# All eight buffers of weight parts at one remainder of 256 bytes, and four buffers of weight sums for five

## The chip, the core and the metric

The kernel runs on one core of a Trainium2 chip. TensorE (PE in the profile; PEld are its weight loads) multiplies, VectorE (DVE), ScalarE (ACT) and GpSimd (POOL) do the rest on data in SBUF, and SyncE (SP) issues the transfers. The metric is the time of one execution on the device in microseconds (us), smaller being better. Of the kernel before there are three timed runs, 553.04, 554.88 and 555.45 us, with a median of 554.88, and one profiled execution.

## The reference

```python
def reference(q, k, v, w_gate, w_val, w_out, rms_g, w_in, w2_out):
    # q, k, v: 2 batches x 12 heads x 448 x 64
    scores = where(causal, q @ k.T / 8, -1e9)
    attn = exp(scores - max(scores)); attn = attn / (sum(attn) + 1e-9)
    x = (attn @ v) laid out as 896 tokens x 768
    xn = x / sqrt(mean(x * x) + 1e-6) * rms_g
    g = xn @ w_gate                       # 768 x 1536
    x = (silu(g) * (xn @ w_val)) @ w_out  # 1536 x 768
    h = maximum(x @ w_in, 0)              # 768 x 2048
    return (h * h) @ w2_out               # 2048 x 768
```

All arrays are float32; the result is 896 x 768.

## The kernel before

Attention comes first, two heads at a time, in 12 steps. Then three matrix stages follow: the gated one (`w_gate`, `w_val`), its output product (`w_out`), and the second layer's two products (`w_in`, `w2_out`). Activations are kept transposed, features on the 128 partitions and 448 tokens of one batch as columns.

**Parts.** TensorE multiplies float32 operands rounded to its shorter form (F32R). To keep float32's accuracy, each operand is split into a high part (the rounded number) and a low part (what is left). A product of a weight tile and an activation tile is then three matmuls, high x high, high x low, low x high (line 691, in `product`). Every one loads 128 x 128 weights and streams 448 columns. Activation parts are tiles called `part`; weight parts are tiles called `ring`, of which there are eight buffers, each with the high and the low part of up to three weight tiles. `form` fills a ring buffer: the high part by ACT or POOL (lines 267 and 265), the low part by DVE or POOL (line 676).

**Sums.** Pairs of output tiles go through a scheme with seven products in place of eight (`halves`); it needs sums and differences of weight quarters (`minus`, line 703), which are kept in buffers called `st`, of which there are five. A second place that writes `st` is line 649, which puts a weight's number together from what was transferred (`raw`).

**Order.** All steps are recorded first. A planner (`Order`) with assumed costs and due times then picks the engine of each and the order on each engine, and hands out buffers: a step that needs a new `ring` or `st` gets the free buffer that has been free for longest. Semaphore waits follow from that: whoever writes a buffer anew waits for the last reader of what was in it.

**Places in SBUF.** A buffer's place is fixed when its pool first hands it out. In front of the rings lie two `raw` (6,144 bytes per partition each) and one `wt` (3,072); the rings begin at byte 33,024, which is 129 x 256, with the second `wt` between the second and third ring. A ring buffer has 6 x 128 + 16 words, 3,136 bytes, of which the first `o` = 14 words (56 bytes) are skipped. In a row, the parts of the eight buffers begin at these remainders of 256:

| ring buffer | 1 | 2 | 3 | 4 | 5 | 6 | 7 | 8 |
|---|---|---|---|---|---|---|---|---|
| before | 56 | 120 | 184 | 248 | 56 | 120 | 184 | 248 |
| after | 252 | 252 | 252 | 252 | 252 | 252 | 252 | 252 |

The six weight tiles in a buffer are 512 bytes apart, and so at the same remainder. All `part` tiles begin at a multiple of 256, and the low half of each does too (448 x 4 = 7 x 256).

Of the kernel before, what the change touches and what calls it, by code (L numbers as in the profile page):

```python
# [8 lines left out]
F32 = mybir.dt.float32  # L9
F32R = mybir.dt.float32r  # L10
BF16 = mybir.dt.bfloat16
U32 = mybir.dt.uint32
# [7 lines left out]
P = 128  # L20
# [166 lines left out]
def tile_attention_moe_moe2(ctx: ExitStack, tc: tile.TileContext, qk, v, wg, wv, wo, w2i, w2o, rms_g, out):  # L187
# [16 lines left out]
    pw = ctx.enter_context(tc.tile_pool(name="pw", bufs=1))  # L204
# [5 lines left out]

    shapes = dict(raw=([P, 6 * P, 2], U32), wt=([P, 6 * P], F32), st=([P, 3 * P], F32), ring=([P, 6 * P + 16], F32R),
                  snap=([P, S], F32), tt=([P, S], F32), uu=([P, S], F32), part=([P, 2, S], F32R), row=([P, S], F32),
                  s=([P, 1024], F32))
    order = Order(dict(qk=3, v=3, p1=2, p2=2, pt=2))
# [2 lines left out]
    def have(pool, **n):  # L219
        for name, k in n.items():  # L220
            for _ in range(k):
                i = len(order.places.get(name, ()))

                def make(name=name, i=i):
                    t = pool.tile(shapes[name][0], shapes[name][1], tag=f"{name}{i}", name=name, bufs=1)
                    if name == "ring":

                        o = 14
                        t = t[:, o:o + 6 * P].rearrange("p (a k n) -> p a k n", a=2, k=3)
                    return t  # L230

                order.more(name, make)

    def banks(name, *which):
        for i in which:
            order.more(name, lambda i=i: psum.tile([P, 512], F32, tag=f"b{i}", name=name, bufs=1))
# [1 line left out]
    have(psum, s=2)  # L238
    banks("t", 0, 1, 2)
    banks("o", 3)  # L240
    have(pw, raw=2, wt=2, st=5, ring=8)
    have(pt_, snap=5, tt=2, uu=2, part=6, row=14)


# [863 lines left out]
```

## Time and profile before

| | |
|---|---|
| median of three timed runs | 554.88 us (553.04 to 555.45) |
| the profiled execution | 552.39 us, of which the span is 550.6 |
| PE busy, PEld busy | 540.0 us (98%), 474.2 (86%) |
| DVE, ACT, POOL busy | 419.0 (76%), 411.3 (75%), 294.1 (53%) |
| L691 matmuls | 2,115 |
| chain that ended last | PE 75%, DVE 8%, ACT 2% |

How to read it: the page gives busy time per engine and the groups of instructions that cost most, each with its line, its tiles (written <- read), its count, the mean of one in ns, and the idle time in front of it. The chain of waits follows the work that ended last back from the end of the program, so its pieces in order of time tell which engine held the end at each moment. PE's matmul durations overlap one another; the distance from one weight load to the next is the better measure of PE's pace.

### The profile page before, as it was taken

What the parts mean: (1) busy time and instruction counts of PE and PEld (TensorE: products, weight loads), DVE (VectorE), ACT (ScalarE), POOL (GpSimd) and SP (SyncE); (2) the same over time, 40 slices, a digit from 0 to 9 for tenths busy, and PEclk for the clock granted to TensorE, in tenths of its full rate; (3) what the DMA queues carried; (4) which work ended last, traced back from release to release, by engine and by line L of the source; (5) the groups of instructions that cost most, each with busy time, mean ns of one, the idle gap of its engine ahead of it and who ended that gap; (6) DMA issues with size and microseconds to landing.
All of it is one profiled execution on the core that took longest, in us unless ns stands there. A gap on an engine that the chain in (4) does not pass through costs nothing.

```text
span 550.6 us, 8918 instructions
## 1 busy us (share of the span) xinstructions
PE 540.0 (98%) x3067; PEld 474.2 (86%) x3067; DVE 419.0 (76%) x781; ACT 411.3 (75%) x879; POOL 294.1 (53%) x338
## 2 busy tenths in 40 slices
PE   7999999999999999999999999999999999999997
PEld 4766666798899999999999989999999999999996
DVE  4667868699998787879867877996777544778873
ACT  4889998556867766679878777888888998759610
POOL 4546556314331452248999698231113897899610
PEclk9999999999999999999999999999999999999999
DMA  7256513123153333333544143144332343333422
GB/s 184 86 160 210 161 46 107 37 80 114 59 169 118 116 115 115 119 118 110 179 126 146 64 174 115 58 141 146 114 117 77 114 155 112 116 115 122 148 78 83
DMA packets 19501, 65.06 MB, mean 118 GB/s; under 512 B 2048, under 2 KB 8960, under 8 KB 19456
## 3 DMA queue, kind: packets, MB, share of 16 engines
q1 hardware_dynamic: 19376, 64.27, 35.9%
q8 instruction: 24, 0.39, 0.3%
q10 hardware_dynamic: 80, 0.23, 0.1%
q14 instruction: 21, 0.17, 0.1%
HBM read 61.74 MB, written 2.75 MB: 117 GB/s over the span
## 4 chain that ended last, share of the span: by engine, by line
PE 75%; DVE 8%; ACT 2%; issue 1%; POOL 0%; DVEq 0%; ACTq 0%; POOLq 0%
PE m L691 71%; DVE part L559 2%; DVE ring L676 2%; PE s L895 1%; PE o L510 1%; PE t L472 1%; DVE row L723 1%; DVE s L649 1%; DVE row L611 1%; PE s L359 0%; DVE row L838 0%; ACT p2t L430 0%; DVE row L816 0%; ACT part L267 0%; DVE mx L405 0%
## 5 line engine op out<-in xcount | busy, mean ns | idle before, releaser
L691 PE MATMUL m<-part,ring 128*128 128x448 f32 x2115 | 432.9, 366 | 0.4 <-ACT ring L267 0.2
L691 PEld LDWEIGHTS m<-part,ring 128*128 128x128 f32 x2115 | 396.6, 188 | 36.6 <-ACT ring L267 0.6
L559 POOL TENSOR_TENSOR part<-row,part 128x448 fp32r<-128x448 f32 x103 | 120.4, 1193 | 52.0 <-ACT part L267 50.3
L676 DVE TENSOR_TENSOR ring<-s,ring 128x384 fp32r<-128x384 f32 (+1 forms) x156 | 82.4, 542 | 41.1 <-ACT ring L267 40.4
L267 ACT CAST ring<-s 128x384 fp32r<-128x384 f32 (+1 forms) x156 | 71.9, 474 | 29.5 <-PE m L691 20.0
L267 ACT CAST part<-row 128x448 fp32r<-128x448 f32 x131 | 69.1, 569 | 6.2 <-DVE row L611 2.6
L723 POOL TENSOR_TENSOR row<-row 128x448 f32<-128x448 f32 x57 | 66.7, 1185 | 13.1 <-DVE row L835 12.3
L644 ACT ACTIVATE raw<-raw 128x768 uint32<-128x768 uint8 (+1 forms) x70 | 62.5, 897 | 11.5 <-DMA raw<-in_w2o 4.6
L265 POOL TENSOR_SCALAR ring<-st 128x384 fp32r<-128x384 f32 x14 | 7.7, 548 | 104.9 <-DVE st L703 55.7
L639 ACT ACTIVATE s<-raw 128x768 f32<-128x768 f32 (+1 forms) x64 | 54.2, 855 | 6.9 <-DVE ring L676 5.7
L649 DVE SCALAR_TENSOR_TENSOR s<-s,raw 128x768 uint32<-128x768 uint32 (+1 forms) x64 | 48.8, 762 | 9.6 <-ACT s L639 4.9
L676 POOL TENSOR_TENSOR ring<-st,ring 128x384 fp32r<-128x384 f32 x45 | 38.5, 870 | 7.2 <-ACT ring L267 6.1
L267 ACT CAST ring<-st 128x384 fp32r<-128x384 f32 x44 | 21.5, 515 | 21.9 <-DVE st L703 16.3
L456 POOL TENSOR_SCALAR p<-p,r 128x128 f32<-128x128 f32 (+1 forms) x48 | 24.1, 521 | 23.6 <-DVE r L446 19.8
L405 DVE TENSOR_REDUCE mx<-s 128x2 f32<-128x256 f32 (+2 forms) x36 | 24.1, 688 | 15.9 <-PE s L375 9.5
L703 DVE TENSOR_TENSOR s<-s,st 128x384 f32<-128x384 f32 x56 | 31.6, 565 | 1.8 <-ACT ring L267 0.3
L456 POOL TENSOR_SCALAR p2t<-p2t,r 128x256 f32<-128x256 f32 (+1 forms) x36 | 23.2, 660 | 17.9 <-DVE r L446 7.7
L703 DVE TENSOR_TENSOR st<-st,s 128x384 f32<-128x384 f32 x56 | 30.5, 545 | 0.1
L981 DVE TENSOR_TENSOR row<-m,row 128x448 f32<-128x448 f32 x36 | 22.3, 618 | 7.8 <-PE m L691 7.6
L359 PE MATMUL s<-qk 64*128 64x128 f32 (+2 forms) x144 | 24.5, 425 | 3.6 <-ACT p L430 1.4
L308 ACT COPY snap<-m 128x448 f32<-128x448 f32 x43 | 22.9, 532 | 6.0 <-PE m L691 5.9
L559 DVE TENSOR_TENSOR part<-row,part 128x448 fp32r<-128x448 f32 x37 | 25.4, 711 | 1.1 <-ACT part L267 1.0
(101 smaller groups left out, 558.1 us busy)
## 6 DMA issues: line engine op xcount, KB each, us to landing
raw<-in_w2i SPq DMA_DIRECT2D x16, 768.0 KB, 4.3
raw<-in_wg SPq DMA_DIRECT2D x12, 768.0 KB, 4.6
raw<-in_wv SPq DMA_DIRECT2D x12, 768.0 KB, 4.2
raw<-in_wo SPq DMA_DIRECT2D x12, 768.0 KB, 4.4
raw<-in_w2o SPq DMA_DIRECT2D x12, 768.0 KB, 4.4
qk<-in_qk SPq DMA_DIRECT2D x11, 448.0 KB, 4.5
raw<-in_w2o SPq DMA_DIRECT2D x6, 512.0 KB, 3.8
out_t<-row SPq DMA_DIRECT2D x12, 224.0 KB, 1.9
```

What stands on the lines that cost most here:

```text
L267: eng.copy(o, i)
L359: nc.tensor.matmul(s[:, h, o:o + n], z["qk"][BOTH[h], 0, qs], z["qk"][BOTH[h], 1, :n], start=True, stop=False)
L405: nc.vector.tensor_reduce(z["mx"][:, k:k + 2], src, AX, ALU.max)
L456: E(e).tensor_scalar(t, t, z["r"][:, k:k + 1], 1.0, ALU.mult, ALU.mult)
L559: E(e).tensor_sub(bs.tile[:, 1], bf.tile, bs.tile[:, 0].bitcast(F32))
L639: nc.scalar.activation(bt.tile[:, :n * P], br.tile[:, :n * P, 1].bitcast(F32), AF.Prelu, scale=2.0 ** -112, alpha=2.0 ** 32)
L644: nc.scalar.activation(br.tile[:, :n * P, 0], b, AF.Copy, scale=1.0 / 32, bias=-31.0 / 64)
L649: nc.vector.scalar_tensor_tensor(dst.tile.bitcast(U32) if dst else u, u, 3, br.tile[:, a:b, 0], ALU.logical_shift_left, ALU.bitwise_or)
L676: E(e).tensor_sub(br.tile[:, 1, :n], num(), br.tile[:, 0, :n].bitcast(F32))
L691: nc.tensor.matmul(bank.tile[:, :S], bw.tile[:, a, i], x[:, c], start=first and i == 0 and k == 0, stop=last and i == n - 1 and k == 2, sk ...
L703: (E(e).tensor_add if plus else E(e).tensor_sub)(bs.tile[:, o:o + 3 * P], x, y)
L723: E(e).tensor_sub(bs.tile, a[0].tile, b[0].tile)
```

## The change

Three numbers change. A ring buffer gets 6 x 128 + 64 words, 3,328 bytes (13 x 256). The first 63 words of it are skipped, 252 bytes, where 14 were. There are four `st` buffers instead of five; eight times 192 bytes more and 1,536 less leave the tiles behind them where they were.

```diff
-ring=([P, 6 * P + 16], F32R),
+ring=([P, 6 * P + 64], F32R),
...
-                        o = 14
+                        o = 63
                         t = t[:, o:o + 6 * P].rearrange("p (a k n) -> p a k n", a=2, k=3)
...
-    have(pw, raw=2, wt=2, st=5, ring=8)
+    have(pw, raw=2, wt=2, st=4, ring=8)
```

On every engine the instructions stand in the same order as before, and read and write tiles of the same names. What differs is on whom DVE waits where a sum gets its buffer. One of these places is this, on DVE in the output product of the gated stage (`st_3308` is a sum of weights, `m`, `row`, `snap` belong to results; the number behind a semaphore's name is its own):

```order
 L676 TENSOR_TENSOR ring_3284<-s_3237,ring_3284 128x384 [waits PE_49]
 L703 TENSOR_TENSOR st_3304<-st_3277,s_3263 128x384 [waits DVE_49]
-L703 TENSOR_TENSOR st_3308<-st_3304,s_3237 128x384 [waits DVE_49]
+L703 TENSOR_TENSOR st_3308<-st_3304,s_3237 128x384 [waits DVE_49,Pool_49]
 L703 TENSOR_TENSOR s_3237<-s_3237,st_3308 128x384 [waits DVE_49]
-L981 TENSOR_TENSOR row_3327<-m_3169,snap_3182 128x448 [waits PE_49,Pool_49]
+L981 TENSOR_TENSOR row_3327<-m_3169,snap_3182 128x448 [waits PE_49]
 L676 TENSOR_TENSOR ring_3340<-s_3263,ring_3340 128x384 [waits Activation_49]
```

Nothing moved; the sum `st_3308` now waits for POOL, which has read its buffer's former content, and the later row no longer has to.

## Rows read from the trace of the kernel before

**Rows 1.** The page: busy us, share, instructions; granted clock in 40 slices
```profile
PE 540.0 (98%) x3067; PEld 474.2 (86%) x3067; DVE 419.0 (76%) x781; ACT 411.3 (75%) x879; POOL 294.1 (53%) x338
...
PEclk9999999999999999999999999999999999999999
```

**Rows 2.** The chain of waits in time: start us, us, what
```profile
109.07 1.27 DVE row L611 x2
...
145.75 161.93 PE m L691 x792
...
308.25 0.96 DVE s L649
...
317.27 0.97 DVE s L649
...
318.89 226.21 PE m L691 x1107
...
547.21 0.62 DVE row L981
```

**Rows 3.** Groups of PE's weight loads: busy us, mean ns, idle before
```profile
L691 PEld LDWEIGHTS m<-part,ring 128*128 128x128 f32 x2115 | 396.6, 188 | 36.6 <-ACT ring L267 0.6 <-ACT part L267 0.5 <-DVE ring L676 0.4
```

**Rows 4.** Timeline, weight loads of one remainder: start us, us, what, count
```profile
200.76 3.59 PEld L691 LDWEIGHTS m<-part,ring 128*128 128x128 f32 x18
...
526.23 3.70 PEld L691 LDWEIGHTS m<-part,ring 128*128 128x128 f32 x18
...
541.02 3.70 PEld L691 LDWEIGHTS m<-part,ring 128*128 128x128 f32 x18
...
370.25 3.70 PEld L691 LDWEIGHTS m<-part,ring 128*128 128x128 f32 x18
...
362.85 3.66 PEld L691 LDWEIGHTS m<-part,ring 128*128 128x128 f32 x18
...
357.33 3.65 PEld L691 LDWEIGHTS m<-part,ring 128*128 128x128 f32 x18
```

**Rows 5.** Timeline, weight loads behind three restarts at remainder 248
```profile
132.99 1.20 PEld L691 LDWEIGHTS m<-part,ring 128*128 128x128 f32 x6
...
138.12 1.60 PEld L691 LDWEIGHTS m<-part,ring 128*128 128x128 f32 x8
...
145.72 1.90 PEld L691 LDWEIGHTS m<-part,ring 128*128 128x128 f32 x10 [0.49 <-ACT part L267]
...
146.03 1.59 PEld L691 LDWEIGHTS m<-part,ring 128*128 128x128 f32 x8
```

**Rows 6.** Timeline, last readers of two sum buffers and their next writers
```profile
361.72 0.55 DVE L676 TENSOR_TENSOR ring<-st,ring 128x384 fp32r<-128x384 f32 x1
...
369.94 0.55 DVE L703 TENSOR_TENSOR st<-st,s 128x384 f32<-128x384 f32 x1
...
266.08 1.69 POOL L676 TENSOR_TENSOR ring<-st,ring 128x384 fp32r<-128x384 f32 x2 [1.13 <-ACT ring L267]
...
275.38 0.55 DVE L703 TENSOR_TENSOR st<-st,s 128x384 f32<-128x384 f32 x1
```

**Rows 7.** Tile ring, its writers: duration ns min/median/max, first and last start
```profile
L676 DVE TENSOR_TENSOR ring<-s,ring x156: 281/549/561, 132.3 to 532.8; 128x384 fp32r<-128x384 f32 x150, 128x128 fp32r<-128x128 f32 x6
...
L676 POOL TENSOR_TENSOR ring<-st,ring x45: 857/869/946, 153.1 to 528.8; 128x384 fp32r<-128x384 f32 x45
```

**Rows 8.** Windows: us, then busy us (instructions) of PE PEld DVE ACT POOL
```profile
119.00:160.00 41.00, 40.84 (x199) 36.83 (x198) 40.86 (x75) 29.94 (x57) 15.24 (x13) 1.00 0.28 97
...
308.00:318.90 10.90, 10.65 (x54) 9.54 (x52) 10.87 (x18) 8.17 (x16) 6.91 (x7) 1.00 0.37 114
```

**Rows 9.** Timeline, a low part by DVE and the loads of its group
```profile
338.66 0.56 DVE L676 TENSOR_TENSOR ring<-s,ring 128x384 fp32r<-128x384 f32 x1
...
339.06 1.82 PEld L691 LDWEIGHTS m<-part,ring 128*128 128x128 f32 x9
```

More of the change, by code (lines that the diff above doesn't have):

```diff
@@ L209, in tile_attention_moe_moe2 @@
     atc = att.enter_context(tc.tile_pool(name="atc", bufs=1))
-    shapes = dict(raw=([P, 6 * P, 2], U32), wt=([P, 6 * P], F32), st=([P, 3 * P], F32), ring=([P, 6 * P + 16], F32R),
+    shapes = dict(raw=([P, 6 * P, 2], U32), wt=([P, 6 * P], F32), st=([P, 3 * P], F32), ring=([P, 6 * P + 64], F32R),
                   snap=([P, S], F32), tt=([P, S], F32), uu=([P, S], F32), part=([P, 2, S], F32R), row=([P, S], F32),
```

## The prediction

> **What bounds the kernel now.** I read the page's busy shares first: TensorE (PE) is busy 98% of the span and its granted clock is full, the higher of its two levels (2.4 GHz), in all 40 slices [rows 1]. So either its instructions become shorter or the span stays. The chain of waits in order of time says where that holds [rows 2]. From 109.07 us up to 145.75 the chain runs over VectorE (DVE), with a few ScalarE pieces at its end; then 792 matmuls of L691 follow one another for 161.93 us; from 308.25 to 318.3 the chain is on DVE again; then come 1,107 matmuls in 226.21 us, to within 5 us of the end. 1,899 matmuls in 388.14 us is 204.4 ns each, and each nanosecond of that step is worth 1.9 us of the kernel's time. The first stretch has 204.5 ns, the second 204.3.
>
> What is in a step? The group of weight loads [rows 3] has 2,115 loads of 188 ns with 36.6 us idle before them, of which 1.5 us are named waits: some 17 ns of gap stand behind nearly every load. A step is therefore a weight load and a gap, not the stream of 448 columns with something else in its way, and the question is what sets the gap.
>
> The matmuls of the program and the 2,187 load records of L895 and L691 stand in the same order, so each load can be given to its buffer by counting. Of the records of L691, 573 read a buffer that begins 56 bytes behind a multiple of 256, 504 one at 120, 507 at 184 and 531 at 248. A stretch of the timeline in which 18 loads follow one another from buffers of one remainder gives the step: (duration - one load of 0.19) / 17 [rows 4]. At 248 it is (3.59 - 0.19) / 17 = 200.0 ns in the row of 200.76 us, and (3.70 - 0.19) / 17 = 206.5 in those of 526.23 and 541.02 us. At 120 it is 206.5, at 184 204.1, at 56 203.5, each to within 0.6 since rows have two decimals. The operation and shape are one and the same. So the step depends on where the weights lie, and at 248 there are two rhythms: of the 549 loads there (the 18 of L895 among them) 369 stand in the short one and 180 in the long one. In no group of loads that had settled did one rhythm turn into the other, also not where a second group at 248 followed (the rows of 200.76 and 541.02 are each two groups).
>
> **The change part by part.** *The remainder.* A ring buffer grows from 3,136 to 3,328 bytes, which is 13 x 256; those in front of and between the rings (wt, 3,072) are multiples of 256 too, so all eight buffers begin at 63 x 4 = 252. The moving operands (part) stay at a remainder of 0. No row shows weights at 252. The nearest are those at 248, one word in front, in the same 64 bytes; the three other remainders are 64 bytes and more away. Bounds: 200.0 and 206.5 ns, the ends of rows 4, which happen to be the two rhythms of the nearest remainder as well. I take 200.0, for this reason: after a restart of PE the loads at 248 went to the short rhythm each time. Such restarts are at 132.9, near 138.1 and at 145.7 us; (1.20 - 0.19) / 5 = 202, (1.60 - 0.19) / 7 = 201 and (1.59 - 0.19) / 7 = 200.0 ns are what follows, the first two with their first steps in them [rows 5]. The long rhythm was entered only from groups at another remainder, and after the change there are none. The sum: 1,899 x (204.4 - 200.0) = 8.4 us less.
>
> What the trace says against a plain rule: the Trainium skill (SBUF — State Buffer, "Who interferes with whom") says "PE and ACT never wait on anyone", and TensorE: Matmul & The Clock Gate ("Back-to-back issue gap") lets the spacing depend on the two operations and the free size alone. By these the address is no matter and the change is worth 0. The trace disagrees, with 200.0 and 206.5 ns for one shape. That page's formula for a single gap, N / 2.4 + 2.5, gives an estimate of 189 ns for 448 columns, and the sum by it would be 29 us less; no stretch of this trace has it.
>
> *What the suppliers take back.* Shorter steps pay only while weights and parts keep up. From 119 to 160 us DVE is busy 40.86 of 41 us [rows 8], so ahead of 145.75 I count nothing. From 308 to 318.9 us it is busy 10.87 of 10.9; PE has 54 matmuls there, and would only wait longer, 0.24 us that are not in the 8.4 anyway. DVE's start into that piece, at 308.25, comes right behind work on PE's results, so it moves forward with PE. The tightest supply that I found in the stretches of PE is a low part that DVE ends at 338.66 + 0.56 = 339.22; the third load of its group, which reads it, is at 339.06 + 2 x 0.2045 = 339.47 [rows 9]. By then PE has won 100 x 4.4 ns = 0.44 us since 318.89, against 0.25 of lead: 0.2 us. There are a few more with a lead near 1 us. Nothing and 1.5 us bound it; I take 0.6.
>
> *Four buffers of sums for five.* No instruction moves on any engine; what changes is which buffer a sum is written to, and so on whom the writer waits. For each of these writes I looked up in this trace when the last reader of its new buffer ends. The tightest: DVE reads a sum until 361.72 + 0.55 = 362.27 and its buffer is written at 369.94, 7.7 us later. The tightest behind GpSimd (POOL): two low parts from 266.08, of which the first reads the buffer and ends 0.87 later, 266.95; the write is at 275.38, 8.4 us later [rows 6]. PE's gain inside a stretch is at most 8.4 us in all and moves readers and writers alike. Cost 0; if that cover were gone, DVE would wait in front of a sum with the subtractions for the next rings behind it, and PE would wait for those.
>
> *Writers of the rings.* ScalarE, DVE and POOL write them at an odd word now. The four remainders of today lie in one row for each engine, and DVE's half of them keep to 549 ns between 281 (the six small ones) and 561; POOL's are 857 to 946 [rows 7]. An odd word is not shown. The rows bound it by 0 and by the spread among whole tiles, some 90 ns for POOL's 45, 4 us of an engine that idles 256 us of the span. I take 0, since they lie beside PE's stretches.
>
> Sum: 8.4 - 0.6 = 7.8 us. The profiled execution took 552.39 us (a span of 550.6 and 1.8 around it), 2.5 less than the median of 554.88 and 0.7 less than the fastest of the three. 544.6 by the profile, 547.1 against the median.
>
> **The rivals.** *Locked in the long rhythm (slower).* One remainder for all cuts both ways: what PE falls into at 145.7 us it keeps until the next restart at 318.9, and what it falls into there, to the end. At 206.5 ns the two stretches cost 1,899 x 2.1 = 4.0 us more: 558.9. For it: 180 loads of 549 at 248 and all that settled at 120. Against it: the three restarts. It decides at the first ten loads after a restart. 17%; some 3% more for a step above 206.5, which no stretch shows.
>
> *A rhythm in between (no change).* 252 is not 248; it may behave as 56 or 184 do, 203.5 to 204.4 ns: a gain of 0 to 1.7 us, 553.2 to 554.9. For it: two of four remainders have no short rhythm. The same result comes if the first stretch locks short and the second long (792 x 4.5 - 1,107 x 2.2 = 1.1 us less, 553.8). 19%.
>
> *The address is no matter.* The step stays at a mean of 204.4 and the time at 554.9. Rows 4 stand against it. 3%.
>
> *Short in the long stretch alone.* 1,107 x 4.3 = 4.8 less, 792 x 2.0 = 1.6 more for the first: 551.7. 5%.
>
> **How the numbers follow.** The forecast, 547.1 us, has 53%; its own range is 545 to 550, from nothing taken back by suppliers and a gain in a few of the loads ahead of 145 us, up to 3 us taken back. About 0.5%, 2.8 us here, can be told from no change, so faster means below 552.1 and slower above 557.7. Faster: 53 + 5 = 58%. Same: 19 + 3 = 22%. Slower: 20%. The range of 8 in 10 must take in the middle cases and most of the long rhythm: 544.5 to 560.
>
> **What would show it.** Stretches of 18 loads at 3.59 us from 146 us on show the short rhythm, 3.70 the long one, 3.65 the middle. The gap in the group of loads should fall from 36.6 us to about 2,115 x 12 ns = 25 us. In the chain, 792 matmuls should take 158.4 us and 1,107 some 221.4. The DVE pieces at 109 to 145 and 308 to 318 should stay, and no POOL release should stand in front of a sum of L703. The prediction fails if loads at 252 settle anywhere but at 200, or if the rhythm changes within a stretch without a restart, or if named waits of L691 grow by several us because suppliers, not PE, set the pace.

## The result and the profile after

Over 16 runs the changed kernel takes 549.57 us in the median (546.25 to 553.35), the kernel before 554.61 (552.11 to 555.58) in its 16. The ratio is 0.9914, with a 95% interval from 0.9896 to 0.9933: 0.9% faster. The single runs of the change lie wider apart, over 7.1 us, than those of before, over 3.5.

The profiled execution of the change is one of its slower ones, 552.47 us, as long as the one of before (552.39). That is no contradiction, and its trace says why. First the page's busy times and granted clock:

```profile
PE 540.6 (98%) x3067; PEld 477.3 (87%) x3067; DVE 420.2 (76%) x781; ACT 411.0 (75%) x879; POOL 301.8 (55%) x338
...
PEclk9999989999999999999999999999999999999999
```

The first line answers to [rows 1]: PE is as busy as before. In the second, one slice of the attention steps has a lower digit, which before had not:

```profile
68.00:83.00 15.00, 13.90 (x124) 9.89 (x118) 9.89 (x23) 13.06 (x41) 8.37 (x13) 0.89 0.22 68
```

(columns: the window, its length, busy us and instructions of PE, PEld, DVE, ACT and POOL, then the granted clock.) PE is busy for 13.90 of these 15 us. The mean clock is 0.89 of full there: for part of the time the lower of the two levels (1.2 GHz) was granted. Dips of this kind come and go with both kernels: in the runs beside the last experiments four of nine executions of the kernel before have a mean clock of 0.996 and 554.4 to 555.0 us, five have 0.999 or 1.0 and 551.7 to 553.2. So this execution comes some 2 us late to its long stretch of matmuls, and the one of [rows 2] had the full clock. The dip has a part in the spread of the change's 16 runs too: the six with a mean clock of 0.999 or 1.0 took 546.25 to 549.84 us, the ten with 0.996 or 0.997 took 548.25 to 553.35.

The chain of waits in time, which answers to [rows 2] (start, length, what; the stretch in the middle has many short pieces, of which one is shown):

```profile
148.12 159.06 PE m L691 x792
...
307.74 0.96 DVE s L649
...
318.37 16.47 PE m L691 x81
...
378.30 6.15 DMA raw<-in_w2i
...
386.21 117.17 PE m L691 x567
...
503.49 41.66 PE m L691 x207
...
547.29 0.62 DVE row L981
```

792 matmuls now take 159.06 us where they took 161.93: 200.8 ns each with their waits. The 2.4 us by which the stretch began late are won back, and 0.5 more: the second stretch starts at 318.37 where it started at 318.89. Then PE holds the chain for 81 matmuls only. From 334.86 to 386.21 pieces of DVE, ACT and a weight transfer hold it: PE has overtaken its suppliers. Before, PE held all of this. The 567 matmuls from 386.21 are the surprise, 206.7 ns each (117.17 / 567).

Stretches of the timeline with weight loads, all of them at remainder 252, answer to [rows 4] (start, length, count; the step is the length less one load of 0.19, divided by the count less one):

```profile
163.00 9.99 PEld L691 LDWEIGHTS m<-part,ring 128*128 128x128 f32 x50
...
303.01 3.39 PEld L691 LDWEIGHTS m<-part,ring 128*128 128x128 f32 x17
...
352.08 3.65 PEld L691 LDWEIGHTS m<-part,ring 128*128 128x128 f32 x18
...
384.86 0.79 PEld L691 LDWEIGHTS m<-part,ring 128*128 128x128 f32 x4
...
386.21 1.33 PEld L691 LDWEIGHTS m<-part,ring 128*128 128x128 f32 x7 [0.56 <-ACT snap L308]
...
394.99 10.11 PEld L691 LDWEIGHTS m<-part,ring 128*128 128x128 f32 x49
...
509.97 3.59 PEld L691 LDWEIGHTS m<-part,ring 128*128 128x128 f32 x18
```

At 163 us (9.99 - 0.19) / 49 = 200.0 ns, at 303 likewise (3.20 / 16); at 384.86 still (0.60 / 3); at 395 (10.11 - 0.19) / 48 = 206.7; at 510 (3.59 - 0.19) / 17 = 200.0 again. In between, at 386.21, stands a restart: PE waited 0.56 us for ScalarE. It came out of that wait in the long rhythm and stayed in it for some 520 steps, to 494 us, where one load came 93 ns late, its matmul 2 ns, and the short one took over. Step by step the short rhythm is 199, 203, 198 ns (or 198, 198, 204; mean 200.0), the long one 206, 207, 207. A third rhythm stands behind the restart at 351 us: 33 steps, up to the next wait at 358 us, have a mean of 203.3 ns (the row of 352.08 gives (3.65 - 0.19) / 17 = 203.5). So the forecast, its main rival and, for 7 us, the rhythm in between all happened, in one execution, one behind the other.

The group of loads, answering to [rows 3], and the named waits of L691's loads from 119 us to the end (total us, times, longest):

```profile
L691 PEld LDWEIGHTS m<-part,ring 128*128 128x128 f32 x2115 | 396.9, 188 | 33.8 <-ACT ring L267 1.2 <-ACT snap L308 0.8 <-DVE ring L676 0.6
```

```profile
PEld m L691 <- ACT ring L267: 1.2, 2, 0.7
...
PEld m L691 <- ACT snap L308: 0.8, 2, 0.6
...
PEld m L691 <- DVE ring L676: 0.6, 1, 0.6
...
PEld m L691 <- ACT part L267: 0.6, 1, 0.6
...
PEld m L691 <- ACT snap L770: 0.6, 2, 0.4
...
PEld m L691 <- DVE row L1034: 0.5, 1, 0.5
...
PEld m L691 <- issue: 0.4, 1, 0.4
...
PEld m L691 <- ACT row L1041: 0.4, 1, 0.4
```

The idle time in front of loads fell from 36.6 to 33.8 us, not to 25: 520 x 6.7 ns = 3.5 us of it are the long rhythm, and the waits add up to 5.1 us where they were 1.9, issue counted in both. Last, the writers of the rings, answering to [rows 7]:

```profile
L676 DVE TENSOR_TENSOR ring<-s,ring x156: 280/548/560, 134.7 to 533.1; 128x384 fp32r<-128x384 f32 x150, 128x128 fp32r<-128x128 f32 x6
...
L676 POOL TENSOR_TENSOR ring<-st,ring x45: 1009/1022/1420, 155.5 to 529.9; 128x384 fp32r<-128x384 f32 x45
```

DVE is as before. POOL's subtraction went from a median of 869 ns to 1,022, which neither the prediction's 0 nor its bound of 90 ns had.

### The profile page after: what moved, and what is told of

Read it like the earlier page. It is cut to its first block, busy times and chain, and to the rows that moved or that the text cites. A ratio compares the mean times of both kernels' runs of the same rounds, so it can differ in the third digit from the quotient of the medians.

```text
span 550.7 us, 8919 instructions
## 1 busy us (share of the span) xinstructions
PE 540.6 (98%) x3067; PEld 477.3 (87%) x3067; DVE 420.2 (76%) x781; ACT 411.0 (75%) x879; POOL 301.8 (55%) x338
## 4 chain that ended last, share of the span: by engine, by line
PE 74%; DVE 13%; ACT 6%; DMA 3%; issue 2%; POOL 1%; POOLq 0%; DVEq 0%; ACTq 0%
PE m L691 61%; DVE part L559 3%; PE t L472 3%; PE o L510 3%; PE s L359 3%; DVE ring L676 2%; DMA raw<-in_w2i 2%; PE s L372 2%; DVE row L723 1%; PE s L895 1%; ACT ring L267 1%; ACT p2t L430 1%; DVE s L649 1%; POOL p L456 1%; ACT s L639 1%
## 5 line engine op out<-in xcount | busy, mean ns | idle before, releaser
L691 PE MATMUL m<-part,ring 128*128 128x448 f32 x2115 | 429.4, 365 | 1.4 <-ACT ring L267 0.6
L691 PEld LDWEIGHTS m<-part,ring 128*128 128x128 f32 x2115 | 396.9, 188 | 33.8 <-ACT ring L267 1.2
L676 POOL TENSOR_TENSOR ring<-st,ring 128x384 fp32r<-128x384 f32 x45 | 45.9, 1038 | 5.0 <-ACT ring L267 3.7
L703 DVE TENSOR_TENSOR st<-st,s 128x384 f32<-128x384 f32 x56 | 30.5, 545 | 0.2
L359 PE MATMUL s<-qk 64*128 64x128 f32 (+2 forms) x144 | 26.4, 448 | 1.6 <-ACT p2t L430 1.1
```

The source lines that it names most:

```text
L359: nc.tensor.matmul(s[:, h, o:o + n], z["qk"][BOTH[h], 0, qs], z["qk"][BOTH[h], 1, :n], start=True, stop=False)
L676: E(e).tensor_sub(br.tile[:, 1, :n], num(), br.tile[:, 0, :n].bitcast(F32))
L691: nc.tensor.matmul(bank.tile[:, :S], bw.tile[:, a, i], x[:, c], start=first and i == 0 and k == 0, stop=last and i == n - 1 and k == 2, sk ...
L703: (E(e).tensor_add if plus else E(e).tensor_sub)(bs.tile[:, o:o + 3 * P], x, y)
```

## The experiments

Theory A: the step of a load and its matmul depends on the remainder of the weights' address, with one or more stable rhythms for each; the change puts all loads at one remainder with a rhythm of 200.0 ns. Rival B: that all buffers are alike is what helps, whatever the remainder. Rival C: the sums' buffers carry it. Later came D, that not the weights' remainder counts but its distance from that of the moving operand, with E, the weights' own address, as its rival. Every kernel is written as a difference to the changed one, except the first.

### Four buffers of sums alone

```diff
-    have(pw, raw=2, wt=2, st=5, ring=8)
+    have(pw, raw=2, wt=2, st=4, ring=8)
```

(to the kernel before)

> Four buffers of sums, ring buffers as in the kernel before (remainders 56, 120, 184, 248). Theory A (the gain comes from where the weights lie): no change, 554 to 555 us, loads at the four remainders as before. Rival C (the sums' buffers carry the gain, by other waits): about 549.5 us.

Measured: 554.72 us (10 runs) beside 554.51 (19 runs), ratio 1.0005, 0.9987 to 1.0023. C falls, and the step of the prediction that put this part at 0 stands.

### All at 248

```diff
-                        o = 63
+                        o = 62
```

> All eight ring buffers at remainder 248 in place of 252, one word less. Theory A: the two rhythms known from the kernel before, 200.0 or 206.7 ns, each held from one restart to the next; time between 546 and 556 us by which is held, likeliest 547 to 551. Rival B (what helps is that all buffers have the same remainder, whichever it is): as the changed kernel, 549.5 us, with the same spread.

Measured: 551.64 us, but from 545.9 to 556.9 over 10 runs. The ratio, 0.9927 (0.9896 to 0.9959), is that of the seven shortest alone and so flatters this kernel; the two medians, 551.64 and 554.51, give 0.995. Stretches of its profiled execution, the longest of all, which is in the long rhythm for most of its steps:

```profile
162.91 3.59 PEld L691 LDWEIGHTS m<-part,ring 128*128 128x128 f32 x18
...
180.47 0.71 PEld L691 LDWEIGHTS m<-part,ring 128*128 128x128 f32 x4 [0.37 <-ACT snap L770]
...
200.00 3.70 PEld L691 LDWEIGHTS m<-part,ring 128*128 128x128 f32 x18
...
329.84 3.79 PEld L691 LDWEIGHTS m<-part,ring 128*128 128x128 f32 x19
...
399.97 3.70 PEld L691 LDWEIGHTS m<-part,ring 128*128 128x128 f32 x18
```

200.0 ns at 163 and 330, 206.5 at 200 and 400, and the change at a restart, as at 180.47. Step by step the rhythm holds from 181 to 321 us and from 389 to 549 without one exception. A told the range to within 1 us; it could not tell which of the two each restart picks, and there the reason for taking the short one, "each time" of three restarts, was too little.

### All at 120

```diff
-                        o = 63
+                        o = 30
```

> All eight ring buffers at remainder 120, whose loads settled at 206.7 ns in the kernel before. Theory A: 1,899 steps x 2.3 ns more than before, 558 to 560 us, 206.7 ns from end to end. Rival B (sameness alone): 549.5 us.

```profile
169.86 3.91 PEld L691 LDWEIGHTS m<-part,ring 128*128 128x128 f32 x19
```

Measured: 559.8 us (557.99 to 560.2), ratio 1.0087 (1.0063 to 1.0112), 206.7 ns from end to end, (3.91 - 0.19) / 18. B falls: sameness at the wrong remainder costs 5 us. The slower rival of the prediction had nearly this time, 558.9.

### Eight remainders in one execution, three times

```diff
-                        o = 63
+                        o = 56 + i
...
+                        o = (15, 31, 47, 0, 1, 16, 32, 48)[i]
...
+                        o = 48 + i if i else 8
```

(one line for each of three kernels; `i` is the buffer's number)

> Eight ring buffers at eight remainders, 224 to 252 in steps of one word; one profile shows the rhythm of each, group by group. Theory A: each remainder has rhythms of its own, all between 200 and 207 ns; those from 240 on, next to 248 and 252, have the one of 200. Rival (the remainder counts in whole 64 bytes, so one word is no matter): all eight alike, 200.0 and 206.7 ns in about equal parts. Time 549 to 556 us.

> Eight ring buffers at remainders 60, 124, 188, 0, 4, 64, 128 and 192, parts at 0 as before. Theory A: a rhythm for each, between 200 and 207 ns; no number more exact for any of them. Those at 60, 124 and 188 (one word in front of a multiple of 64) are to be held against 252: if only the place within 64 bytes counted, all four would be bistable at 200.0 and 206.7; the kernel before with 56, 120, 184 and 248 apart speaks against it. Time 549 to 558 us.

> Eight ring buffers at remainders 32 and 196 to 220 in steps of one word. Theory A: rhythms between 200 and 207 ns; the short one of 200.0 at two or three of them at most, since among 224 to 252 it is at 228, 240, 248 and 252 in part of the groups. Rival (short rhythms only just in front of a multiple of 256): none below 203 here. Time 550 to 557 us.

Times: 552.21, 552.34 and 552.99 us, one execution each. Loads were given to their buffers by order again; the means of the last six steps inside each group of nine loads or more, with the number of groups (18 of the 24 remainders; groups with a wait among these six steps are left out):

| remainder | settles at, ns (groups) | remainder | settles at, ns (groups) |
|---|---|---|---|
| 0 | 203 (16), 207 (7), 202 (5) | 212 | 209 (15), 200 (9), 202 (2) |
| 4 | 204 (31) | 216 | 203 to 204 (25), 200 (2) |
| 60 | 202 to 204 (29) | 220 | 203 to 204 (17), 207 (10) |
| 64 | 202 (26) | 224 | 207 (21), 200 (6), 204 (2) |
| 124 | 203 to 204 (26) | 228 | 201 to 202 (26) |
| 188 | 200 (18), 207 (8) | 240 | 203 to 204 (18), 200 (13) |
| 192 | 200 to 201 (28) | 244 | 202 to 205 (26) |
| 200 | 200 to 201 (26) | 248 | 200 to 201 (23), 207 (4) |
| 208 | 202 to 204 (31) | 252 | 200 to 202 (22), 207 (6) |

Some stretches of 18 loads, of the second kernel (remainders 60, 192 and 0) and of the first (224 and 240):

```profile
334.41 3.64 PEld L691 LDWEIGHTS m<-part,ring 128*128 128x128 f32 x18
...
459.92 3.59 PEld L691 LDWEIGHTS m<-part,ring 128*128 128x128 f32 x18
...
464.72 3.70 PEld L691 LDWEIGHTS m<-part,ring 128*128 128x128 f32 x18
```

```profile
334.27 3.70 PEld L691 LDWEIGHTS m<-part,ring 128*128 128x128 f32 x18
...
450.22 3.59 PEld L691 LDWEIGHTS m<-part,ring 128*128 128x128 f32 x18
```

One word makes a difference at many places (240 and 244, 208 and 212), so the rival of whole 64 bytes falls, and so does the one that short rhythms stand only just in front of 256. My own expectation failed at 244, which has no step of 200, and at 212, where most groups settled above 207. Of the third kernel's remainders 200 has the short step in all groups and 212 in some, as expected. New: 192 and 200 showed no rhythm but the short one.

### Parts moved by 64 bytes, rings at 60

```diff
+    pad = pt_.tile([P, 16], F32, name="pad")
+    nc.gpsimd.memset(pad, 0.0)
...
-                        o = 63
+                        o = 15
```

(the pad stands in front of all tiles behind the rings)

> All tiles behind the rings, the parts among them, are moved by 64 bytes, and the ring buffers begin at 60: the distance from part to weight is 252 modulo 256 as in the changed kernel, the remainders themselves are 64 and 60. Theory D (the distance between moving operand and weights counts): the rhythms of the changed kernel, 198-199-203 with a mean of 200.0, and 206.7; 546 to 553 us. Rival E (the weights' own address counts): the rhythm that the scan shows for 60, without one of 198-199-203.

```profile
164.88 3.79 PEld L693 LDWEIGHTS m<-part,ring 128*128 128x128 f32 x19
...
399.84 3.79 PEld L693 LDWEIGHTS m<-part,ring 128*128 128x128 f32 x19
```

Measured: 548.61 us (548.12 to 549.35), ratio 0.9896 (0.9871 to 0.992). All stretches are at 200.0 ns, (3.79 - 0.19) / 18, and step by step 199, 203, 198 or 198, 198, 204, the changed kernel's short rhythm. With parts at 0, weights at 60 settled at 202 to 204 (3.64 above, 203). D holds, E falls. The long rhythm does not occur in this execution, and the four runs lie within 1.2 us; whether that is chance was not shown.

### All at 240

```diff
-                        o = 63
+                        o = 60
```

> All eight ring buffers at 240, where the scan of the last eight words has groups at 200.0 and at 203 ns and none at 206.7. Theory A: every run between 200.0 and 203.3 ns a step, so 547 to 553 us, with less spread from run to run than at 248 or 252 (7 to 11 us). Rival (a remainder's rhythm in a mixture says nothing of the same remainder alone): spread and median as at 252, 549.6 with 7 us.

```profile
164.90 3.79 PEld L691 LDWEIGHTS m<-part,ring 128*128 128x128 f32 x19
...
399.86 3.85 PEld L691 LDWEIGHTS m<-part,ring 128*128 128x128 f32 x19
```

Measured: 551.0 us (549.76 to 552.72), ratio 0.9931 (0.9907 to 0.9955). Steps of 200.0 ns and of (3.85 - 0.19) / 18 = 203.3, no third; 3.0 us of spread over 5 runs where 252 had 7.1 over 16. What the mixture showed of 240 holds for it alone.

### All at 192, and all at 200

```diff
-                        o = 63
+                        o = 48
...
+                        o = 50
```

> All eight ring buffers at 192, where in the scan every one of 27 groups settled at 200.0 ns (201-197-202). Theory A with one rhythm only: 200.0 from end to end whatever the restarts do, 545.5 to 548 us in every run, and so faster than 252 by about 2 to 3 us in the median and with a spread under 3 us. Rival (a long rhythm that the mixture did not show, as 252 alone has): 549.5 us with a spread of 7.

> All eight ring buffers at 200, where 26 groups of the scan settled at 200 to 201 ns. As for 192: 545.5 to 548 us in every run if the short rhythm is the only one; 549.5 with a spread of 7 if there is a long one.

One stretch at 192, then two at 200, then the chain of waits at 200:

```profile
400.00 3.59 PEld L691 LDWEIGHTS m<-part,ring 128*128 128x128 f32 x18
```

```profile
164.92 3.59 PEld L691 LDWEIGHTS m<-part,ring 128*128 128x128 f32 x18
...
399.95 3.79 PEld L691 LDWEIGHTS m<-part,ring 128*128 128x128 f32 x19
```

```profile
147.23 70.74 PE m L691 x351
...
217.97 88.60 PE m L691 x441
...
317.77 180.35 PE m L691 x900
...
498.18 41.66 PE m L691 x207
```

Measured: 547.22 us at 192 (546.65 to 548.42), ratio 0.9884 (0.986 to 0.9909), and 546.72 at 200 (545.96 to 548.19), ratio 0.9873 (0.9844 to 0.9902); of before, 553.2. 200.0 ns everywhere, before and behind every restart; in the chain 900 matmuls in 180.35 us, 200.4 each with their waits. With one rhythm the restarts no longer decide the time: the five runs lie within 1.8 us at 192 and 2.2 at 200. The best of the kernels tried is the one at 200; its interval and that of the change overlap by a little (0.9902 against 0.9896), so that it beats the change is likely and not settled.

### Parts moved by 64 bytes, rings at 252 and at 0

```diff
+    pad = pt_.tile([P, 16], F32, name="pad")
+    nc.gpsimd.memset(pad, 0.0)
...
-ring=([P, 6 * P + 64], F32R),
+ring=([P, 6 * P], F32R),
...
-                        o = 63
+                        o = 0
...
-    have(pw, raw=2, wt=2, st=4, ring=8)
+    have(pw, raw=2, wt=2, st=5, ring=8)
```

(the first of the two kernels has the pad alone)

> Rings at 252 as in the changed kernel, the tiles behind them, parts among them, moved by 64 bytes: the distance from part to weight is 188. Theory D (the distance counts): the rhythms that the scan has for 188, flat 200-200-200 or 207, and no 198-199-203. Rival E (the weights' own address): 198-199-203 and 206-207-207. Time 546 to 556 us.

> Rings at 0 without any word in front (3,072 bytes each), five buffers of sums again, and the tiles behind the rings moved by 64 bytes: the distance from part to weight is 192. Theory D: the rhythm of 192, 201-197-202 with a mean of 200.0, and the time of all rings at 192, 545.5 to 548 us in every run. Rival E: the rhythm of 0 in the scan, 203 and 207 ns, and 552 to 559 us.

```profile
164.88 3.79 PEld L693 LDWEIGHTS m<-part,ring 128*128 128x128 f32 x19
...
249.94 3.70 PEld L693 LDWEIGHTS m<-part,ring 128*128 128x128 f32 x18
...
445.01 3.59 PEld L693 LDWEIGHTS m<-part,ring 128*128 128x128 f32 x18
```

```profile
164.84 3.79 PEld L693 LDWEIGHTS m<-part,ring 128*128 128x128 f32 x19
...
399.95 3.79 PEld L693 LDWEIGHTS m<-part,ring 128*128 128x128 f32 x19
```

The first: 552.58 us, one execution; the settled steps are a flat 200, 200, 200 ns or 206, 207, 207 (from 203 to 389 us), never 199-203-198, as 188 has it. The second: 548.39 us (547.95 to 548.63), ratio 0.9903 (0.988 to 0.9926), 200.0 ns throughout in the steps 201, 197, 202 of 192; with parts at 0, weights at 0 settle at 202 to 203 or 207. D holds twice more. Four of the five times are up to 0.6 us over what was expected; all five runs have a mean clock of 0.996 or 0.997, as only two of the five at 192 do. It needs 64 bytes instead of the change's 1,536 and all five sums.

## Why the prediction was right, and what in it was off

*PE's step bounds the kernel, and it hangs on where the weights lie.* Shown: between all at 120 and all at 200, with the same instructions, lie 2.1% by the ratios, 12 us. The kernels with moved parts show more exactly that it is the distance from part to weight. So the rival that the address is no matter falls. The prediction had drawn it in part from the sentence of the Trainium skill (SBUF — State Buffer, "Who interferes with whom") that PE never waits on anyone. That sentence is about engines in each other's way, which no run here tests; the 200.0 and 206.7 ns go by the places of PE's own two operands and do not contradict it.

*252 has the short rhythm of 248.* Right: 200.0 and 206.7 ns, as there, and one stretch of 203.3. The rival with a rhythm in between had more rows for it than the prediction says: three of the four remainders (56, 120, 184) lack a short one, not two. *PE falls into the short one after a restart* was too strong. It held in the first stretch; in the profiled execution the restart at 351 us went to 203.3 ns and the one at 386 to 206.7, and at 248 those at 180 and 389 went to the long one. The prediction had the lock, but as one choice for a whole stretch, 53% against 17%. In fact a run makes several: restarts at 181, 256, 351, 358 and 386 us are among the new ones, and one load late by 0.1 us (494 us) can be enough. So most runs lie between the forecast and the rival, and the median is 549.57.

By its own signs of being wrong the prediction failed on this step: in the profiled execution loads at 252 settled at 206.7 and 203.3 ns, a rhythm changed without a named wait (494 us), and the named waits grew by several us. That the median still lies in the range of 545 to 550 is in part luck. The forecast of 547.1 was for the short rhythm alone; a mixture of rhythms, chosen anew at many restarts, which no term of its sum has, ended 0.4 us below the upper end. What sets the share of each rhythm in a run was not found out.

*Suppliers take back 0.6 us, 1.5 at most.* Mis-sized: named waits grew by 3.2 us, and with 200.0 ns from end to end (all at 200) they are still 4.2 where before had 1.9. PE caught up with DVE and ACT between 335 and 386 us, where the trace of before has PE waiting nowhere. The one lead that the prediction priced, 0.25 us at 339 us, cost nothing, as no wait stands there after the change; the waits came elsewhere, 11 in place of 4.

*Four sums for five cost nothing.* Right, by the first experiment.

*Writers at an odd word cost nothing.* Wrong by 153 ns for each of POOL's 45 subtractions, 7.4 us of its time; the bound was 4. The odd word is not the reason either: POOL is as slow at 192, an even word, and fast at 4, an odd one (last section). What it adds to the time was not separated: 192 (1,031 ns) and 200 (869 ns) differ by 0.5 us, inside their intervals.

*The sum.* 7.8 us was forecast. With the short rhythm held throughout, at 200, the ratio of 0.9873 is 7.0 us of 553.2; the change itself has 4.8 of 554.6, as the long rhythm takes part of its time.

## What to carry to other kernels

Where PE does nothing but load weights and multiply, look at the distance from load to load, buffer by buffer: a mean of 204 ns can hide four different steps. Weights and moving operands are a pair: their distance modulo 256 bytes sets the step here, and one pad tile moves it. Try eight distances in one execution, one per buffer, and take one that settles at a single short step, since one with two makes the time a matter of chance.

## What the runs showed of the hardware

For 128 columns of weights and 448 moving columns, the step settled between 200.0 and 209 ns by the distance of the two addresses modulo 256, one word being enough to change it. The distance was told from the address by moving the parts once, by 64 bytes. Several distances have two stable rhythms, 252 in one stretch a third; in the profiles of 252, 248, 240 and 188 each change from one to another stood behind a wait of PE or a matmul that came 2 to 21 ns late. The commonest settled means, 200.0, 203.3 and 206.7 ns, are 30, 30.5 and 31 times 6.67 ns; whether that means anything was not found out, nor what the distance does.

POOL's subtraction of 128 x 384 words took 864 to 874 ns where the ring's part began 4 or 8 bytes behind a multiple of 16 (12 remainders, 4, 196, 200 and 248 among them), and 1,016 to 1,031 where it began at 0 or 12 (15 remainders, 0, 60, 192 and 252 among them), medians for each remainder; DVE's and ACT's times for the same tiles did not change with it.
